# Late-row projections at the start, feed-forward pairs inside the recurrence, and another order of weight loads in a fused attention and feed-forward kernel

## The chip, the cores and the metric

The kernel runs on one core of a Trainium2 chip. The metric is device time in microseconds, as the median of several runs. Times inside the kernel come from one execution that was recorded by the hardware profiler; they count from the start of its span. The engines are TensorE (PE, with its weight loads PEld), VectorE (DVE), ScalarE (ACT), GpSimd (POOL) and SyncE (SP), which issues most of the DMAs.

## What is computed

A layer norm, an attention with a small memory that is handed from segment to segment, a residual, a second layer norm, a gated feed-forward part and a second residual. S = 2048 rows of width 640, 32 heads of 128, segments of 32 rows, 8 memory rows, feed-forward width F = 1728, all in bf16.

```python
def A(x, mem0, Wq, Wk, Wv, Wo, seg_len):              # x is the normalised input
    mem = mem0
    for s in range(64):
        h = concat([mem, x[:, 32*s:32*s+32]])         # 8 + 32 rows
        q, k, v = (einsum('btd,dhe->bhte', h, w) for w in (Wq, Wk, Wv))
        p = softmax(where(mask, q @ k.T * 128**-0.5, -1e9))
        o = einsum('bhte,hed->btd', p @ v, Wo)
        mem = o[:, :8]                                # the next segment needs this
        outs.append(o[:, 8:])
    return concat(outs)

def B(x, W_gate, W_up, W_down):
    gate = x @ W_gate
    return ((gate * (gate > 0)) * (x @ W_up)) @ W_down

h   = x + A(layernorm(x), ...)
out = h + B(layernorm(h), ...)
```

## The kernel before

**Order.** Every instruction is recorded by `add(engine, function, r=keys read, w=keys written)` and every DMA by `dma(...)`. `solve` turns the keys into semaphore waits; each engine then runs its own instructions in the recorded order. So the order of the source is the order of each queue, and an instruction that waits holds up all that stand behind it on its engine. DMAs go to SyncE's queue unless another engine is named. A key such as `("Wdone", 1)` stands for the last use of a weight matrix, after which its memory holds something else. `dma` issues at L349, DMA transposes at L372.

**The opening.** The weights W (Q, K and V, 15 chunks of 1 MB, in the order K, Q, V) and then Wo (8 loads) are read into SBUF. Meanwhile TensorE projects what it has: for K and Q three passes over each chunk (rows of segments 0 and 1, first group of late rows, memory and rows of segment 0), for V two (`first_values`). `keep_busy(n)` (L967) is n dummy matmuls into a bank that nothing reads. After the V chunks comes segment 0, and then the V projection of one more group of late rows into `Ve[0]`.

**The recurrence.** Steps 1 to 63 each do one segment: project the 8 memory rows with 24 of its own rows to K, Q and V (`project`: 40 products of 32 x 512 for each matrix, four of them side by side on TensorE's column groups, L411), scores (L507), softmax, values for the memory rows (`pv_mem`, L560), the output projection of the memory rows in two parts (L623 and L606) and their transposition into the next step's input. The values of the other rows (`pv_x`, L695) follow one step later. The last 8 rows of each segment, called late rows here, don't fit the 32-column pass; they are projected for four segments at once, one matrix a step, in `extra_units`: in steps r = 0, 1, 2 of each group of four the matrices K, Q, V go to `Ke`, `Qe`, `Ve` of the next group (two buffers each; buffer 1 of all three lies in `ends`). For the group of segments 58 to 61 these are steps 54, 55 and 56. The projection is cut into parts that fill places where TensorE would wait (`filler`).

**Feed-forward pairs inside the recurrence.** The first 512 rows are normalised and transposed early and kept in DRAM (`xn2_d`). In steps 58, 59 and 60, where no late rows are left to project, `early_product` computes one pair each (128 columns of gate and of up for the 512 rows, ten products of 128 x 512, L835), and stores the result in DRAM (`hx_d`). NE = 3 is their number. Rows lie in `ends`, the gate weights in `xt`, the up weights in `xl`.

**Splits.** `fill_of(s)` says how many of a step's projection matmuls are cut in two halves of 256 columns or load their weights again. This changes the number of TensorE's instructions in a step, not what is computed.

**The last part.** When the recurrence ends, the memory of W takes the feed-forward weights (`Wg`, `Wu`, `Wd`, the 64 tail columns `Wt`), rows and products. The pieces of `Wg` and `Wu` are listed in `pieces` by column groups and are loaded one by one by `load_piece(key)`, which waits for `("Wdone", 0)` and the key that is given; `load_down(n, p)` loads three row chunks of `Wd` and waits for the chunk NE + p of `hT`. Four blocks of 512 rows follow. A block has 13 pairs and a tail (`gate_up`, L835, L931, tail L944), then two pairs of down products (L1207, L384, L1220). Block 0 takes its first NE chunks of `hT` from `hx_d`; its next four pairs lie between the remains of steps 62 and 63, the rest behind. Rows of the next block are read, added to the attention (`ln2_front`, VectorE) and transposed by DMA (`ln2_back`) while a block runs.

## Time and profile before

| what | us |
|---|---|
| median of 3 runs | 995.79 (995.68 to 996.4) |
| the profiled execution, its time | 996.75 |
| its span | 995.0 |
| opening, up to the first output projection of segment 0 (L623) | 47.91 |
| output projection (L623) of step 1, of step 2 | 66.39, 78.59 |
| output projection of step 62 | 802.23 |
| first pair of block 0 after the recurrence's products (L835) | 810.75 |
| first down product of block 0 (L1207) | 842.93 |
| first pair of block 1 (L931) | 858.08 |

A step is 12.05 us in the mean ((802.23 - 66.39) / 61 = 12.06), and a block 44.25 us (858.08 to 902.32). The granted TensorE clock is 1.00 in nearly all stretches.

The table is read by stages: up to about 41 us the DMA engines are full with weights (share 1.0 at 411 to 425 GB/s), then come 62 steps in which TensorE is never idle for more than 0.1 us after step 2, then a stretch from 805 to 858 us in which weights are loaded again, and three equal blocks.

### The profile page before, as it was taken

What the parts mean: (1) busy time and instruction counts of PE and PEld (TensorE: products, weight loads), DVE (VectorE), ACT (ScalarE), POOL (GpSimd) and SP (SyncE); (2) the same over time, 40 slices, a digit from 0 to 9 for tenths busy, and PEclk for the clock granted to TensorE, in tenths of its full rate; (3) what the DMA queues carried; (4) which work ended last, traced back from release to release, by engine and by line L of the source; (5) the groups of instructions that cost most, each with busy time, mean ns of one, the idle gap of its engine ahead of it and who ended that gap; (6) DMA issues with size and microseconds to landing.
All of it is one profiled execution on the core that took longest, in us unless ns stands there. A gap on an engine that the chain in (4) does not pass through costs nothing.

```text
span 995.0 us, 56316 instructions
## 1 busy us (share of the span) xinstructions
PE 968.9 (97%) x26093; PEld 530.3 (53%) x24848; DVE 711.5 (72%) x1856; ACT 521.7 (52%) x1324; POOL 167.6 (17%) x412
## 2 busy tenths in 40 slices
PE   4799999999999999999999999999999999999998
PEld 1145555555555555555555655656565564444443
DVE  2468787878887887888788878787877865545332
ACT  1356666666666666666666666656665542122120
POOL 7011202021312130213022202021210010000000
PEclk9999999999999999999999999999999999999999
DMA  9941112121222122212212131112123259613100
GB/s 369 416 142 36 51 32 54 28 54 50 59 45 54 48 54 42 55 53 49 48 47 54 48 55 41 44 46 41 40 62 79 78 146 267 143 20 97 24 14 27
DMA packets 79105, 77.40 MB, mean 78 GB/s; under 512 B 45322, under 2 KB 64786, under 8 KB 76946
## 3 DMA queue, kind: packets, MB, share of 16 engines
q1 hardware_dynamic: 77136, 72.84, 26.4%
q8 instruction: 200, 3.28, 1.4%
q10 hardware_dynamic: 1730, 0.96, 0.4%
q14 instruction: 39, 0.32, 0.1%
HBM read 39.91 MB, written 7.74 MB: 48 GB/s over the span
## 4 chain that ended last, share of the span: by engine, by line
PE 94%; DMA 3%; DVE 1%; SPq 1%; issue 0%; ACT 0%; POOL 0%; DVEq 0%; ACTq 0%; POOLq 0%
PE ps L411 47%; PE ps L931 10%; PE ps L384 8%; PE ps L606 7%; PE ps L623 7%; PE ps L666 4%; PE ps L1207 3%; DMA W<-in_A_Wv_dram 3%; PE ps L507 2%; PE ps L695 2%; PE ps L560 2%; PE ps L835 2%; SPq L349 1%; PE ps L944 0%; PE ps L1220 0%
## 5 line engine op out<-in xcount | busy, mean ns | idle before, releaser
L411 PE MATMUL ps<-W,act_r 128*32 128x512 bf16 (+1 forms) x8301 | 453.8, 358 | 1.2 <-DVE act_r L647 0.8
L411 PEld LDWEIGHTS ps<-W,act_r 128*32 128x32 bf16 x8301 | 212.5, 96 | 165.9 <-DVE act_r L647 31.6
L435 ACT ACTIVATE tok<-ps 128x512 bf16<-128x512 f32 x186 | 107.2, 594 | 56.5 <-PE ps L411 48.6
L411 PE MATMUL ps<-W,act_e 128*32 128x512 bf16 x1152 | 112.8, 384 | 6.6 <-DMA W<-in_A_Wv_dram 4.1
L430 DVE STREAM_TRANSPOSE Ko<-tox 128x512 bf16<-128x512 bf16 x128 | 89.6, 701 | 40.9 <-ACT tox L435 40.7
L435 ACT ACTIVATE tox<-ps 128x512 bf16<-128x512 f32 x134 | 79.7, 598 | 65.1 <-PE ps L411 44.9
L586 DVE STREAM_TRANSPOSE oT<-tox 128x512 bf16<-128x512 bf16 x128 | 94.5, 738 | 0.0
L430 DVE STREAM_TRANSPOSE Qo<-tok 128x512 bf16<-128x512 bf16 x124 | 85.4, 689 | 0.8
L606 PE MATMUL ps<-Wo,oT 128*32 128x160 bf16 x4032 | 81.5, 233 | 0.0
L623 PE MATMUL ps<-Wo,oT 128*32 128x320 bf16 x2016 | 79.8, 299 | 0.6 <-DVE rm L570 0.6
L384 PE MATMUL ps<-W,act_e 128*32 128x512 bf16 x808 | 79.8, 385 | 0.0
L606 PEld LDWEIGHTS ps<-Wo,oT 128*32 128x32 bf16 x4032 | 70.3, 97 | 11.1 <-DVE oT L580 3.1
L435 ACT ACTIVATE Vp<-ps 128x512 bf16<-128x512 f32 x127 | 75.1, 592 | 0.5 <-ACT Vp L435 0.5
L636 ACT ACTIVATE SA<-TA 64x40 f32<-64x40 f32 x126 | 29.5, 234 | 75.2 <-DVE TA L634 74.5
L959 ACT ACTIVATE g<-ps 128x512 bf16<-128x512 f32 x49 | 28.3, 593 | 75.8 <-PE ps L931 74.1
L523 ACT ACTIVATE Pm<-ps 128x64 bf16<-128x64 f32 x126 | 28.2, 224 | 73.6 <-PE ps L507 73.6
L960 DVE TENSOR_TENSOR hT<-g,ps 128x512 bf16<-128x512 bf16 x49 | 33.6, 687 | 40.3 <-PE ps L931 35.5
L623 PEld LDWEIGHTS ps<-Wo,oT 128*32 128x32 bf16 x2016 | 52.7, 96 | 16.7 <-DVE rm L570 1.3
L580 DVE STREAM_TRANSPOSE oT<-om 128x128 bf16<-128x128 bf16 x126 | 39.0, 309 | 31.2 <-ACT om L572 31.1
L507 PE MATMUL ps<-Qo,Ko 128*32 128x40 bf16 x2048 | 61.0, 181 | 0.0
L507 PEld LDWEIGHTS ps<-Qo,Ko 128*32 128x32 bf16 x2048 | 46.2, 94 | 25.6 <-DVE Qo L430 18.1
L1207 PE MATMUL ps<-Wd,hT 128*128 128x320 bf16 (+4 forms) x225 | 57.9, 299 | 1.7 <-DVE hT L954 1.7
(131 smaller groups left out, 1441.1 us busy)
## 6 DMA issues: line engine op xcount, KB each, us to landing
VM<-Vp SPq DMA_DIRECT2D x126, 65.0 KB
VM<-Vp SPq DMA_DIRECT2D x63, 130.0 KB
W<-in_A_Wk_dram SPq DMA_DIRECT2D x5, 1024.0 KB
W<-in_A_Wq_dram SPq DMA_DIRECT2D x5, 1024.0 KB
W<-in_A_Wv_dram SPq DMA_DIRECT2D x5, 1024.0 KB
Wo<-in_A_Wo_dram SPq DMA_DIRECT2D x8, 640.0 KB
attn_d<-wtok SPq DMA_DIRECT2D x248, 7.5 KB
xt<-in_A_x_dram SPq DMA_DIRECT2D x16, 160.0 KB
```

The lines of the kernel that those rows point to most:

```text
L384: return pe.add_instruction(mybir.InstMatmult(name=nc.get_next_instruction_name(), engine=mybir.EngineType.PE, ins=[pe.lower_ap(rhs), pe.l ...
L411: ins = pe.matmul(*b, start=(c == ends[0]), stop=(c == ends[1]), skip_group_check=True)
L430: add("dve", lambda v: v.transpose(dst[:, 16 * i:16 * i + 16, 0:32], tok[t][:, :].rearrange("p (h f) -> p h f", f=32)), r=tok_keys(t), w=keys)
L435: add("act", lambda a: a.activation(dst, src, ACTF.Copy), r=r, w=w)
L507: i = pe.matmul(bank((P0, P1)[hf])[q:q + 32, o:o + 40], (Ko if a == 0 else Ke[p])[:, h, :], Qo[:, h, :], start=True, stop=True, skip_group ...
L580: add("dve", lambda v: v.transpose(ap(oT[par], 160 * hf, [[40, 4], [320, 4], [1, 8]]), ap(om, 128 * hf, [[1, 4], [4, 32]])), r=[("om", hf) ...
L586: add("dve", lambda v, kh=kh: v.transpose(ap(oT[p], 160 * kh + M, [[320, 4], [40, 4], [1, 32]]), ap(tox, 128 * kh, [[256, 4], [1, 4], [4, ...
L606: i = pe.matmul(bank(bk)[32 * gg:32 * gg + 32, 0:160], src[:, hb, 0:32], w[:, gg], start=(hb == CH[16 * halves[0]]), stop=(hb == CH[-1]), ...
L623: i = pe.matmul(bank(bk)[32 * q:32 * q + 32, 0:320], src[:, hb, 0:32], w, start=(n == 0), stop=(n == 7), skip_group_check=True)
L666: ins = pe.matmul(bank(bk)[32 * q:32 * q + 32, 0:320], src[:, hb, 0:32], w[:, 2 * (q % 2):2 * (q % 2) + 2], start=(i == 0), stop=(i == 15) ...
L931: ins = pe.matmul(bank(bk), w[:, c, lo:lo + 128], xn2T[par][:, c, :], start=(c == 0), stop=(c == DC - 1))
L1207: i = pe.matmul(*a, start=(j == 0), stop=(j == FC - 1), skip_group_check=True)
```

## The change

Five things change.

1. K and Q of the late rows of segments 58 to 61 are projected in the opening (`next_pass`, two passes of 40 products of 32 x 512). For this the 32 rows are loaded into `xl` ahead of the Q weights, normalised and transposed on TensorE; the results are flipped into `Ve[0]` and `oTe`, saved to DRAM (`next_d`) and loaded into `Ke[0]`, `Qe[0]` in step 56. The ten dummy matmuls go. The load of block 1's rows into `xl` and the copies into `Ve[0]` move behind the saves, and ones are set in `Ve[0]` again.
2. Steps 54 and 55 compute feed-forward pairs instead: NE = 5, `EARLY_STEPS` is (54, 55, 58, 59, 60). Their rows lie in `Ke[0]`, `Qe[0]`, `Ve[0]`, the up weights in `at`. V of these late rows stays in step 56.
3. With NE = 5 there are four column groups of `Wg` and `Wu` and not five. Pieces and `Wd` loads in the last part wait for the end of W's use alone, and stand earlier. The tail weights are loaded once each and copied on POOL into the second order.
4. In a tail the second half of `g1` has a key of its own.
5. `fill_of`: step 1 has 126 in place of 31, step 54 0 in place of 7, step 55 25 in place of 52.

```diff
-    NE = 3
+    NE = 5
+    next_d = [nc.dram_tensor(f"next{i}_d", [128, 32 * H], BF16) for i in range(2)]
...
+            if j == 1 and c == DC - 1:
+                for e in range(4):
+                    t0 = SEG * (NSEG - 6 + e) + RID
+                    dma(xl[M * e:M * e + M, :], x_ap[t0:t0 + M, :], w=[("xl", e)])
...
-    ln1_load(1, xl, ("xl",))
+    for n, (t, ks) in enumerate(((Ve[0], [("Ve", 0, i) for i in range(2)] + [("Ve1", 0)]), (oTe, [("oTe", q) for q in range(4)]))):
+        held_saves.append((n, t, ks))
...
+    row_moments(xl, ("xl", 0), 32, [("xl", e) for e in range(1, 4)])
+    row_std(32)
+    row_scale(xl, ("xl", 0), 32, xl, ("xl",))
...
+            if j == 0 and c == DC - 2:
+                transpose_rows(xl, ("xl",), 32, P3)
+                copy_op("dve", a2, chunks_of(bank_bf(P3)[:, 0:D])[:, :, 0:32], [B(P3)], k2[:2])
...
-    first_values(range(2))
+    def next_pass(n):
+        j, bks, t = ((1, (P0, P1), 2), (0, (T0, T1), 0))[n]
+        for i in range(2):
+            project(a2, k2, j, (i,), (bks[i],))
+        for i in range(2):
+            to_tok(bks[i], t + i, "act")
+            add("dve", lambda v, i=i: v.transpose(next_home(n)[:, 16 * i:16 * i + 16, :],
+                                                  tok[t + i][:, :].rearrange("p (h f) -> p h f", f=32)),
+                r=tok_keys(t + i), w=held_saves[n][2])
...
+    first_values((0,))
+    next_pass(0)
+    first_values((1,))
+    next_pass(1)
...
-    keep_busy(10)
     first_values((3,))
...
+    wo_pass(0, P3, (1,), (3,))
+    keep_busy(3)
+    for n, t, ks in held_saves:
+        dma(next_d[n][:, :], (ap(Ve[0], 0, [[1, 32 * H]]), oTe[:].rearrange("p h t -> p (h t)"))[n], r=ks, w=[("next", n)])
+    ln1_load(1, xl, ("xl",))
+    to_act_split(1, P3)
     for i in range(2):
         to_v(BQ[i], Ve[0], i, ("Ve", 0), "act")
-    wo_pass(0, P3, (1,), (3,))
-    keep_busy(3)
-    to_act_split(1, P3)
+    add("pool", lambda p: p.memset(ap(Ve[0], Dh, [[VW, 8], [1, VW - Dh]]), 1.0), w=[("Ve1", 0)])
     row_stats(xl, ("xl",), n_rows(1))
...
-            if (s - 2) // 4 + 1 == (NSEG - 2) // 4:
-                return early_product(s, r)
+            if s in EARLY_STEPS:
+                return early_product(s)
...
-        n = {1: 31, 2: 8, 57: 39, 58: 0, 59: 27, 60: 40, 61: 39, 62: 50, 63: 0}.get(s, FILL[s % 4])
+        n = {1: 126, 2: 8, 54: 0, 55: 25, 57: 39, 58: 0, 59: 27, 60: 40, 61: 39, 62: 50, 63: 0}.get(s, FILL[s % 4])
...
+            elif s == NSEG - 8:
+                for n, t in enumerate((Ke[0], Qe[0])):
+                    dma(t[:].rearrange("p h t -> p (h t)"), next_d[n][:, :], r=[("next", n)],
+                        w=[(("Ke", "Qe")[n], 0, i) for i in range(2)])
+                add("pool", lambda p: p.memset(ap(Ve[0], Dh, [[VW, 8], [1, VW - Dh]]), 1.0),
+                    w=[("Ve1", 0), ("Ve", 0, 0), ("Ve", 0, 1)])
...
-            if s == NSEG - 7:
-                early_weights(0, 0)
+            if s in (NSEG - 11, NSEG - 7):
+                early_weights(s + 1, 0)
                 G.ops[-1].after = first_exp
-                early_rows(2, 4)
+                early_rows(s > NSEG - 8, 2, 4)
...
-        r = [("Wdone", 1), ("hT", 0, NE + p)]
+        r = [("Wdone", 1)]
...
-    load_piece(("VM", 0, 3))
-    load_piece(("hT", 0, NE))
+    for _ in range(4):
+        load_piece(("Wdone", 0))
     rows(P3, s % 2, s - 1)
     gate_up(0, NE + 1)
+    for n in range(2):
+        load_down(n)
...
+    dma(hT[0][:, 0:NE, :], hx_d[:, :, :], r=[("Wdone", 2)] + [("hx", n) for n in range(NE)],
+        w=[("hT", 0, n) for n in range(NE)])
+    load_down(2)
     gate_up(0, NE + 3)
-    load_piece(("hT", 0, NE + 3))
-    dma(hT[0][:, 0:NE, :], hx_d[:, :, :], r=[("Wdone", 2), ("hT", 0, NE + 3)] + [("hx", n) for n in range(NE)],
-        w=[("hT", 0, n) for n in range(NE)])
-    load_down(0, 3)
-    load_down(1, 3)
+    for q, src in enumerate((B_W_gate, B_W_up)):
+        dma(Wt[:, 0, :, FR * q:FR * q + FR], src[:, FM:F].rearrange("(c p) f -> p c f", p=128), r=[("Wdone", 0)],
+            w=[("Wt", q, 0)])
+        add("pool", lambda o, q=q: o.tensor_copy(Wt[:, 1, :, FR * (1 - q):FR * (2 - q)], Wt[:, 0, :, FR * q:FR * q + FR]),
+            r=[("Wt", q, 0)], w=[("Wt", q, 1)])
+    load_down(3)
     rows(P2, (s + 1) % 2, s)
     ln2_load(5)
+    load_down(4)
...
-            if b == 0 and p in (8, 9):
+            if b == 0 and p in (7, 8):
                 load_piece(("hT", 0, j))
                 load_piece(("hT", 0, j))
             if b + 1 < NBLK:
-                fronts, backs = ((4, 6), (7, 9)) if b == 0 else ((1, 3, 5, 7), (3, 5, 7, 9))
+                fronts, backs = ((4, 6), (6, 8)) if b == 0 else ((1, 3, 5, 7), (3, 5, 7, 9))
```

More of the change, by code (lines that the diff above doesn't have):

```diff
@@ L748, in ln2_back @@
         flip_rows(xn2T[par][:, :, 128 * u:128 * u + 128], xt2[u], ("xt2", u), ("xn2", par, u))
+    held_saves = []
     x0 = oTe[:].rearrange("p h t -> p (h t)")[:, 0:D]
@@ L790, in build_kernel @@
     OB = {1: (BQ, (T0, T1), (P2, P3)), 0: ((P0, P1), BQ, (T0, T1)), 2: ((P2, P3), BQ)}
+    a2, k2 = act_r[1][:, 2], [("act", 1, 2, "m"), ("act", 1, "x", 2), ("act", 1, "x")]
     for j in (1, 0):
@@ L808, in first_values, with next_home @@
                 project(a, ks, 2, (0, 1), bks, (c,))
-    first_values(range(2))
+    def next_pass(n):
[7 more added lines that the diff above has]
+                r=tok_keys(t + i), w=held_saves[n][2])
+    def next_home(n):
+        return (ap(Ve[0], 0, [[32, H], [1, 32]]), oTe)[n]
+    first_values((0,))
+    next_pass(0)
+    first_values((1,))
+    next_pass(1)
     EC = 128 * NE
-    GROUPS = ((EC, EC + 256), (EC + 256, EC + 512), (EC + 512, EC + 1024), (EC + 1024, FM), (0, EC))
+    GROUPS = [(EC, EC + 256), (EC + 256, EC + 512), (EC + 512, EC + 1024), (0, EC)]
+    if EC + 1024 < FM:
+        GROUPS.insert(3, (EC + 1024, FM))
     pieces = [(t, n, src, g, lo, hi) for g, (c0, c1) in enumerate(GROUPS)
               for n, (t, src) in enumerate(((Wg, B_W_gate), (Wu, B_W_up)))
-              for lo, hi in (((0, 3), (3, DC)) if g in (2, 4) else ((0, DC),))]
+              for lo, hi in (((0, 3), (3, DC)) if g in (2, len(GROUPS) - 1) else ((0, DC),))]
     def group_of(j):
@@ L829, in build_kernel, with flat_half @@
     END_KEYS = [("Ke", 1, 0), ("Ke", 1, 1), ("Qe", 1, 0), ("Qe", 1, 1), ("Ve", 1, 0), ("Ve", 1, 1), ("Ve1", 1)]
-    XHOME = [(ends[:, 512 * c:512 * c + 512], END_KEYS[c]) for c in range(DC)]
-    HOME, HKEY = ends[:, 64 * H + 4 * VW + 8:64 * H + 4 * VW + 520], END_KEYS[DC]
+    VHOME = 4 * VW + 8
+    def flat_half(t, i):
+        return t[:].rearrange("p h t -> p (h t)")[:, 512 * i:512 * i + 512]
+    XHOME = [[(flat_half((Ke[0], Qe[0])[c // 2], c % 2), (("Ke", "Qe")[c // 2], 0, c % 2)) for c in range(4)] +
+             [(ap(Ve[0], 0, [[1, 512]]), ("Ve", 0, 0))],
+             [(ends[:, 512 * c:512 * c + 512], END_KEYS[c]) for c in range(DC)]]
+    HOME = [(ap(Ve[0], VHOME, [[1, 512]]), ("Ve", 0, 1)), (ap(Ve[1], VHOME, [[1, 512]]), ("Ve", 1, 1))]
     def by_groups(pe, dst, w, x, c):
@@ L837, in by_groups, with early_rows, early_tile, early_weights @@
         return ins
-    def early_rows(lo, hi):
-        dma(ends[:, 512 * lo:512 * hi].rearrange("p (c t) -> p c t", t=512), xn2_d[:, lo:hi, :],
-            r=[("xn2_d", u) for u in range(4)], w=END_KEYS[lo:hi] + ([("Ve1", 1)] if hi == DC else []))
-    def early_weights(j, q):
-        t, k, src = ((xt, ("xt",), B_W_gate), (xl, ("xl",), B_W_up))[q]
+    def early_rows(q, lo, hi):
+        ks = [XHOME[q][c][1] for c in range(lo, hi)] + ([("Ve1", q)] if hi == DC else [])
+        if q:
+            dst = ends[:, 512 * lo:512 * hi].rearrange("p (c t) -> p c t", t=512)
+        elif hi == DC:
+            dst = XHOME[0][4][0].rearrange("p (c t) -> p c t", t=512)
+        else:
+            dst = (Ke[0], Qe[0])[lo // 2][:].rearrange("p h t -> p (h t)").rearrange("p (c t) -> p c t", t=512)
+        dma(dst, xn2_d[:, lo:hi, :], r=[("xn2_d", u) for u in range(4)], w=ks)
+    def early_tile(s, q):
+        return ((xt, ("xt",)), (at, ("at",)) if s < NSEG - 7 else (xl, ("xl",)))[q]
+    def early_weights(s, q):
+        (t, k), src = early_tile(s, q), (B_W_gate, B_W_up)[q]
+        j = EARLY_STEPS.index(s)
         dma(chunks_of(t[:, :]), src[:, 128 * j:128 * j + 128].rearrange("(c p) f -> p c f", p=128), w=[k])
-    def early_product(s, n):
+    EARLY_STEPS = (NSEG - 10, NSEG - 9, NSEG - 6, NSEG - 5, NSEG - 4)
+    def early_product(s):
+        n, hp = EARLY_STEPS.index(s), int(s >= NSEG - 6)
+        home, hkey = HOME[hp]
         def mul(q, chunks):
-            t, k = ((xt, ("xt",)), (xl, ("xl",)))[q]
+            t, k = early_tile(s, q)
             def f(pe):
                 for c in chunks:
-                    ins = by_groups(pe, bank(BQ[q]), chunks_of(t[:, :])[:, c, :], XHOME[c][0], c)
+                    ins = by_groups(pe, bank(BQ[q]), chunks_of(t[:, :])[:, c, :], XHOME[hp][c][0], c)
                 return ins
-            add("pe", f, r=[k] + [XHOME[c][1] for c in chunks], w=[B(BQ[q])])
+            add("pe", f, r=[k] + [XHOME[hp][c][1] for c in chunks], w=[B(BQ[q])])
         def part(m):
@@ L861, in evac @@
         def evac():
-            add("act", lambda a: a.activation(HOME, bank(BQ[0]), ACTF.Relu), r=[B(BQ[0])], w=[HKEY])
-            add("dve", lambda v: v.tensor_tensor(HOME, HOME, bank(BQ[1]), ALU.mult), r=[B(BQ[1]), HKEY], w=[HKEY])
-            dma(hx_d[:, n, :], HOME, r=[HKEY], w=[("hx", n)])
+            add("act", lambda a: a.activation(home, bank(BQ[0]), ACTF.Relu), r=[B(BQ[0])], w=[hkey])
+            add("dve", lambda v: v.tensor_tensor(home, home, bank(BQ[1]), ALU.mult), r=[B(BQ[1]), hkey], w=[hkey])
+            dma(hx_d[:, n, :], home, r=[hkey], w=[("hx", n)])
         return part, evac
@@ L951, in gate_up @@
                 add("act", lambda a, r0=r0, r1=r1, sl=sl: a.activation(g1[gi][r1:r1 + FR, sl], bank(bg)[r0:r0 + FR, sl],
-                                                                       ACTF.Relu), r=[B(bg)], w=[("g1", gi)])
+                                                                       ACTF.Relu), r=[B(bg)], w=[("g1", gi, e) if e else ("g1", gi)])
                 h = hT[par][:, j, :].rearrange("p (u e t) -> p e u t", e=2, t=128)[r1:r1 + FR, e]
@@ L956, in gate_up @@
                     bank(bg)[r1:r1 + FR, sl].rearrange("p (u t) -> p u t", t=128), ALU.mult),
-                    r=[B(bg), ("g1", gi)], w=[("hT", par, j)])
+                    r=[B(bg), ("g1", gi)] + [("g1", gi, 1)] * e, w=[("hT", par, j)])
             return
@@ L1048, in build_kernel @@
             held, parts = fill_of(s)
-            if NSEG - 6 < s < NSEG - 3:
-                early_weights(s - NSEG + 6, 1)
+            if s in (NSEG - 10, NSEG - 9, NSEG - 5, NSEG - 4):
+                early_weights(s, 1)
+            elif s == NSEG - 8:
[4 more added lines that the diff above has]
+                    w=[("Ve1", 0), ("Ve", 0, 0), ("Ve", 0, 1)])
             elif s == NSEG - 3:
@@ L1146, in build_kernel @@
         filler(1)
-        if s == NSEG - 7:
-            early_rows(0, 2)
-            early_rows(4, DC)
-            early_weights(0, 1)
-        elif NSEG - 6 <= s < NSEG - 4:
-            early_weights(s - NSEG + 7, 0)
+        if s in (NSEG - 11, NSEG - 7):
+            early_rows(s > NSEG - 8, 0, 2)
+            early_rows(s > NSEG - 8, 4, DC)
+            if s == NSEG - 7:
+                early_weights(s + 1, 1)
+        elif s in (NSEG - 10, NSEG - 6, NSEG - 5):
+            early_weights(s + 1, 0)
         norm_mem(s, 1)
@@ L1260, in down_pair, with load_down @@
             down_store(b, u + q, o[q])
-    def load_down(n, p):
+    def load_down(n):
         lo, hi = 3 * n, min(3 * n + 3, FC - 1)
-        r = [("Wdone", 1), ("hT", 0, NE + p)]
+        r = [("Wdone", 1)]
         dma(Wd[:, lo:hi, :], B_W_down[128 * lo:128 * hi, :].rearrange("(j p) d -> p j d", p=128), r=r, w=[("Wd", n)])
@@ L1295, in build_kernel @@
     late_o(s)
-    load_piece(("hT", 0, NE + 1))
     gate_up(0, NE + 2)
     ln2_load(4)
-    load_piece(("hT", 0, NE + 2))
-    load_piece(("hT", 0, NE + 2))
-    gate_up(0, NE + 3)
-    load_piece(("hT", 0, NE + 3))
-    dma(hT[0][:, 0:NE, :], hx_d[:, :, :], r=[("Wdone", 2), ("hT", 0, NE + 3)] + [("hx", n) for n in range(NE)],
-        w=[("hT", 0, n) for n in range(NE)])
-    load_down(0, 3)
-    load_down(1, 3)
+    if len(GROUPS) > 4:
+        load_piece(("Wdone", 0))
+        load_piece(("Wdone", 0))
+    dma(hT[0][:, 0:NE, :], hx_d[:, :, :], r=[("Wdone", 2)] + [("hx", n) for n in range(NE)],
+        w=[("hT", 0, n) for n in range(NE)])
+    load_down(2)
+    gate_up(0, NE + 3)
+    for q, src in enumerate((B_W_gate, B_W_up)):
[4 more added lines that the diff above has]
+    load_down(3)
     rows(P2, (s + 1) % 2, s)
     ln2_load(5)
+    load_down(4)
     woe_pass(P3, range(16))
@@ L1320, in build_kernel @@
                 gate_up(b, j)
-            if b == 0 and p == 4:
-                for q, src in enumerate((B_W_gate, B_W_up)):
-                    for e in range(2):
-                        r0 = FR * (q ^ e)
-                        dma(Wt[:, e, :, r0:r0 + FR], src[:, FM:F].rearrange("(c p) f -> p c f", p=128),
-                            r=[("Wdone", 0), ("hT", 0, j)], w=[("Wt", q, e)])
             if b == 0 and p in (4, 5):
                 ln2_load(p + 2)
-            if b == 0 and 4 <= p < 7:
-                load_down(p - 2, p)
-            if b == 0 and p == 6:
+            if b == 0 and p == 5:
                 dma(h_rows[0][:, :, :], h_d[:, :].rearrange("(u p) d -> p u d", p=128), r=[("h_d", u) for u in range(4)] +
                     [("Wdone", 1), ("hT", 0, j)], w=[("h", 0, u) for u in range(4)])
-            if b == 0 and p in (8, 9):
+            if b == 0 and p in (7, 8):
                 load_piece(("hT", 0, j))
```

## The prediction

> **What bounds the kernel now.** I read the page first: the busy shares, then the chain that ended last. TensorE is busy 97% of the span and carries 94% of the chain, so a change pays only if it takes TensorE work off the path or closes one of TensorE's few gaps. The line of queue 8 (instruction loads) is used for a rival below.

> ```profile
> span 995.0 us, 56316 instructions
> PE 968.9 (97%) x26093; PEld 530.3 (53%) x24848; DVE 711.5 (72%) x1856; ACT 521.7 (52%) x1324; POOL 167.6 (17%) x412
> q8 instruction: 200, 3.28, 1.4%
> PE 94%; DMA 3%; DVE 1%; SPq 1%; issue 0%; ACT 0%; POOL 0%; DVEq 0%; ACTq 0%; POOLq 0%
> ```

> Then TensorE's timeline at both ends; a bracket is idle time before the line and what ended it. In the opening it waits for each 1 MB chunk of the V weights and fills one wait with ten dummy matmuls (L967 and the L384 after it).

> ```profile
> 33.62 0.40 PE L411 MATMUL ps<-W,act_e 128*32 128x512 bf16 x4 [1.09 <-DMA W<-in_A_Wv_dram]
> 36.01 0.40 PE L411 MATMUL ps<-W,act_e 128*32 128x512 bf16 x4 [1.33 <-DMA W<-in_A_Wv_dram]
> 36.98 0.39 PE L967 MATMUL ps<-W 128*128 128x512 bf16 x1
> 37.21 2.11 PE L384 MATMUL ps<-W 128*128 128x512 bf16 x9
> 40.98 0.40 PE L411 MATMUL ps<-W,act_e 128*32 128x512 bf16 x4 [1.67 <-DMA W<-in_A_Wv_dram]
> ...
> 840.00 1.26 PE L944 MATMUL ps<-xn2T,Wt 128*128 128x256 bf16 x10
> 842.93 0.30 PE L1207 MATMUL ps<-Wd,hT 128*128 128x320 bf16 x1 [1.68 <-DVE hT L954]
> ```

> The last line is TensorE's only gap after step 2. VectorE is named, but the first down product does not read the tail rows; it reads hT 0 to 11 and Wd pieces 0 to 3. In the trace's landing records the last part of Wd piece 3 lands at 842.84, 0.09 us before the matmul: this is a late DMA. SyncE's timeline shows that piece issued only at 836.80.

> Third, VectorE's timeline around 57 us, where step 1 begins: it runs nearly without a break from here to 66 us and TensorE waits for it twice (0.94 us at 66.16, 0.84 at 69.67). So what delays L353 delays everything.

> ```profile
> 57.30 0.20 DVE L647 TENSOR_TENSOR act_r<-TBf,SA 128x40 bf16<-128x40 f32 x1
> 57.77 0.89 DVE L353 BATCH_NORM_STATS2 st<-xl 128x6 f32<-128x320 bf16 x2 [0.27 <-issue]
> 59.57 0.45 DVE L367 TENSOR_SCALAR xl<-xl,mv,rs 128x640 bf16<-128x640 bf16 x1 [0.67 <-ACT rs L360]
> 59.98 1.32 DVE L430 STREAM_TRANSPOSE Ko<-tox 128x512 bf16<-128x512 bf16 x2
> ```

> Last, busy times by stretch. A step is measured from one first L623 matmul to the next: the first two rows end in steps 55 and 56, which hold a projection of late rows, the next two in 59 and 60, which hold a feed-forward pair in the same place. The columns are TensorE, weight loads, VectorE, ScalarE, POOL, clock, DMA share, GB/s; the later rows give only the last three.

> ```profile
> 705.93:717.98 12.05, 12.05 (x394) 7.21 (x373) 9.98 (x26) 7.51 (x19) 1.12 (x3) 1.00 0.11 29
> 717.98:730.03 12.05, 12.05 (x394) 7.14 (x374) 10.04 (x26) 7.51 (x19) 1.10 (x3) 1.00 0.11 30
> 754.13:766.18 12.05, 12.05 (x382) 7.21 (x376) 9.50 (x25) 7.02 (x18) 1.13 (x3) 1.00 0.27 67
> 766.18:778.21 12.03, 12.03 (x386) 7.16 (x382) 9.55 (x25) 7.02 (x18) 1.10 (x3) 1.00 0.28 68
> ...
> 816.00:820.00 4.00, 1.00 0.50 146
> 820.00:824.00 4.00, 1.00 0.78 230
> 824.00:828.00 4.00, 1.00 0.98 279
> 828.00:832.00 4.00, 1.00 1.02 358
> ```

> **Part 1: two pairs leave block 0.** With NE=5 the last part computes 8 full pairs of block 0, not 10. Six pairs there run from 827.04 to 840.00: 12.96 / 6 = 2.16 us each, with no gap. Two pairs: -4.32 us.

> **Part 2: the gap before the down products.** Before, each weight piece waits on SyncE's queue for a finished hT chunk; the DMA engines are half idle at 816 to 820. After, four pieces and Wd 0, 1 are issued behind the VM copies (814.4), and Wd 2 and 3 wait for no hT. Ahead of and with Wd 3 stand 1.31 MB pieces, 1.97 MB Wd, 0.66 MB hT rows, 0.33 MB x and attention rows, 0.16 MB tail weights: 4.4 MB. At 325 GB/s (mean of 822 to 832) from 816.5 that is 830. Two of the four tail loads remain; they ran with others at 132 GB/s in 832 to 836, so I add 2 us, and 1.3 us for the slowest DMA engine (it is so much behind at 55 us): Wd 3 lands at 833.5. TensorE ends the tail matmuls at 841.26 - 4.32 = 836.9. VectorE has hT 11 by 834.4 (it comes ahead of the second row front, which ends at 837.3) and hT 12 at 838.0, wanted at 840.1. So the gap goes: -1.68 us (ends: 0 and -1.68). Next due is block 1 at 836.9 + 15.15 = 852.1: its last transposed rows. VectorE finishes the last two row fronts at about 841.6 and 844.4; issue to landing was 4.5 us before, so 849, 3 us early. POOL's two copies of tail weights have that engine free. The finer g1 key shortens the tail's VectorE work behind TensorE: 0.

> **Part 3: steps 54 and 55.** A pair has the same ten 512-column products as the projection it replaces; the rows above say 12.05 against 12.05 and 12.03 (and steps 54 and 58, by their L623 starts, 12.19 and 12.15). The loads go where steps 57 to 59 have theirs. Tightest is the up weight in step 54: it stands on SyncE's queue behind the stores whose issue ends at 700.5, POOL has freed `at` at 698.0, issue to landing takes 2.7 to 3.6 us (the loads of 746.1 and 759.86), so 704.1; TensorE wants it at 705.7. Behind it wait the VM copies, wanted a step later. I take 0 (ends -0.1 and +1). The two reloads and the memset of step 56 have 12 us on queues that are 11% busy: 0. Step 1's fill only halves matmuls; steps with fills 56 and 52 last as long (12.06, 12.05), and VectorE sets step 1: 0 (ends 0 and +1).

> **Part 4: the opening.** Two projections are 20 groups of four at 0.215 us: 4.3 us. They lie in the waits for weights: 1.09 + 1.33 + 1.67 us idle and 2.34 us of dummy matmuls, which go. K starts after chunk 0 (34.5 to 36.7), chunk 1 moves to 36.7 to 37.5, Q takes 37.5 to 39.7; chunk 3 lands at 40.9. Cost 0, with 1.2 us to spare; without cover it would be 4.3. ScalarE and VectorE have four copies (0.6 us) and flips (0.7 us) more, in a stretch where ScalarE idles 7.6 us up to 42.34 and VectorE 6.65 up to 42.66: 0. The 32 extra rows are 41 KB ahead of the Q and V weights: at 424 GB/s +0.1 us.

> **Part 5: the rows of block 1 come later.** Two stores of 262 KB now stand ahead of `xl` on SyncE's queue, behind Wo. In the landing records the last parts are at 56.19 (Wo), 56.59 (xl) and 58.55 (the 0.79 MB of ends_d, so 403 GB/s). The stores add 2 x 0.65 us: xl at 57.9, with the 0.1 at 58.0; L353 starts at 58.1 instead of 57.77: +0.3 us (ends 0 and +5.7, see the third rival). ScalarE's V copies wait for the first store (56.9) and end at 58.1, before L358 needs it at 59.2.
> [...]

> **Sum:** -4.32 - 1.68 + 0 + 0.1 + 0.3 = -5.6 us. The profiled execution (span 995.0, time 996.75) would have a span of 989.4. The median of the runs shown is 995.79, 0.96 under the profiled one; the difference carries over: **990.2 us**.

> **Rivals.** *The DMA engines set the tail.* Their share is 0.9 to 1.46 from 836 to 852. If the same bytes end no earlier, Wd 3 still lands at 842.8, both gains are lost and only the opening's 0.4 remains: 996.2. Against it: the idle share at 816 to 824 and two strided loads fewer. Half of it gives 993.
> *The instruction stream loses its phase* (slower). 51,319 TensorE instructions (matmuls, weight loads, 378 others) in 200 packets on queue 8 are 257 each. TensorE's weight loads idle 183 times, 48.2 us in all, for nothing but "issue", 0.26 us each and about three times a step; no matmul gap goes with it now. If one a step came to lie on the matmuls' path, 61 x 0.26 = +15.9 us, less 5.6: 1006. It decides from 0.09 us a step. Against it: in the two programs' instruction lists TensorE's count at each step from 1 to 53 and from 56 on is exactly 256 higher after, one packet; that is what step 1's fill does.
> [...]
> *The stores drain slowly.* If each took the 3.4 us that the hx_d store of 759.46 takes to land, one after the other, xl would come at 56.2 + 6.8 + 0.4 = 63.4, L353 5.7 us late: 995.9, no change. A quarter of it: 991.5. Against: 403 GB/s of ends_d.

> **Chances.** Forecast 0.77; a part of the stores' delay (991.5) 0.09; half of the DMA rival (993) 0.05; all of it, or of the stores (996), 0.05; phase 0.04. What this measurement can tell from no change is about 0.2%, 2.0 us. Faster is the first three, 0.91; same 0.05; slower 0.04. The range goes from 989.0 (the sum, 0.3 less in the opening, 0.9 for the 0.4 us that runs differ and small gaps) to 993.2, which takes in the partial cases.

> **What would show it.** Right: block 0's down products start about 6 us earlier against step 62 and with no gap ahead; L353 starts 0.2 to 0.6 us later against the Wv chunk; steps 54 and 55 keep 12.05 to 12.2. Wrong: a DMA gap at the first down product or at block 1's first pair; TensorE idle at the up product of step 54; ScalarE held at the V copies past 59 us; a longer step all along.

## The result, and the profile after

The seven runs of the changed kernel have a median of **993.00 us** (990.55 to 993.68), seven of the kernel before on the same chip 995.79 (995.26 to 996.40). The ratio is 0.9965, with a 95% interval of 0.9953 to 0.9977. The forecast was 990.2 with a range of 989.0 to 993.2.

The profiled execution has a span of 989.0 (forecast 989.4) and a time of 990.74, 6.0 under the profiled one of before (forecast 5.6). The seven times lie apart: 990.55, 990.74, 991.77 and then 993.00 to 993.68. So there are two questions: did the profiled 6.0 come from where the prediction put them, and what are the 2.5 us that four of the seven runs take on top. The lines that answer to those of before, from the page of the changed kernel first:

```profile
span 989.0 us, 56556 instructions
PE 964.6 (98%) x26166; PEld 532.7 (54%) x24973; DVE 713.7 (72%) x1861; ACT 522.5 (53%) x1326; POOL 169.6 (17%) x416
q8 instruction: 201, 3.29, 1.4%
PE 93%; DMA 4%; DVE 1%; SPq 1%; issue 0%; ACT 0%; POOL 0%; DVEq 0%; ACTq 0%; POOLq 0%
```

TensorE is busy 4.3 us less: the two pairs. Its timeline in the opening and at the first down product, then VectorE's where step 1 begins (start, length, idle time before and what ended it in brackets):

```profile
33.18 0.40 PE L412 MATMUL ps<-W,act_e 128*32 128x512 bf16 x4 [1.09 <-DMA W<-in_A_Wv_dram]
34.04 2.34 PE L412 MATMUL ps<-W,act_r 128*32 128x512 bf16 x40
36.20 0.40 PE L412 MATMUL ps<-W,act_e 128*32 128x512 bf16 x4
37.06 2.35 PE L412 MATMUL ps<-W,act_r 128*32 128x512 bf16 x40
41.10 0.40 PE L412 MATMUL ps<-W,act_e 128*32 128x512 bf16 x4 [1.69 <-DMA W<-in_A_Wv_dram]
...
836.57 1.26 PE L998 MATMUL ps<-xn2T,Wt 128*128 128x256 bf16 x10
837.66 0.30 PE L1271 MATMUL ps<-Wd,hT 128*128 128x320 bf16 x1
```

```profile
57.79 0.89 DVE L354 BATCH_NORM_STATS2 st<-xl 128x6 f32<-128x320 bf16 x2 [0.23 <-DMA xl<-in_A_x_dram]
59.59 0.45 DVE L368 TENSOR_SCALAR xl<-xl,mv,rs 128x640 bf16<-128x640 bf16 x1 [0.67 <-ACT rs L361]
```

The two new projections (the x40 groups) fill the wait for the second chunk and part of that for the third. The down product follows the tail matmuls without a bracket. L354 now does wait for the `xl` transfer, but starts 0.02 us later than before, no more.

Marked off by the same events in both traces, the 6.0 us are:

| stretch | before | after | difference |
|---|---|---|---|
| start to step 62's first row product | 802.23 | 803.45 | +1.22 |
| from there to the first full pair of block 0 | 24.81 | 24.55 | -0.26 |
| the full pairs of block 0 (6 and 4) | 12.96 | 8.57 | -4.39 |
| tail matmuls and gap, to the first down product | 2.93 | 1.09 | -1.84 |
| from there to VectorE's last operation | 148.94 | 148.94 | 0.00 |
| from there to the end (last store) | 3.16 | 2.41 | -0.75 |

(The first full pair of after lacks one matmul record; its start is put 0.16 us, one matmul, before the first recorded one.) The second row of -0.26 was not followed up. The last row is not a quicker store: in both kernels the last store lands 1.5 us after VectorE's last operation. Behind it SyncE works through its waits for 24 DMA semaphores (the loop over `G.dma_end` at the end of the kernel), 0.06 us apart in its records. The last store has the fifth of them before and the eighteenth after, so 19 waits stand behind it before and 6 after, about 0.78 us less.

The +1.22 is not the opening: step 1's first row product is at 66.45 instead of 66.39. Counted by the first row product (L624) at which they end, steps 12, 28 and 44 take 12.35 to 12.37 us instead of 12.06, together 0.9; steps 54 and 56 take 0.15 more. The timeline of the changed kernel, all engines, shows ahead of 199.73, where step 12 ends, what the 0.3 is:

```profile
188.97 0.40 POOL L596 COPY oTe<-oT 128x256 bf16<-128x256 bf16 x1
189.22 0.48 ACT L637 ACTIVATE SA<-TA 64x40 f32<-64x40 f32 x2 [1.22 <-DVE TA L635]
...
190.13 0.27 POOL L639 TENSOR_TENSOR SA<-SA,TA 128x40 f32<-128x40 f32 x1 [0.76 <-DVE TBf L647]
...
190.50 0.20 DVE L648 TENSOR_TENSOR act_r<-TBf,SA 128x40 bf16<-128x40 f32 x1 [0.38 <-POOL SA L639]
...
190.76 0.51 PE L412 MATMUL ps<-W,act_r 128*32 128x512 bf16 x8 [0.17 <-DVE act_r L648]
```

POOL's addition (L639) reads `SA`; ScalarE is done with it at 189.70. The addition starts 0.43 us after that. In the kernel before, the same two stand at 189.64 and 189.77, 0.13 apart. Everything behind it, down to TensorE, shifts by the 0.3. This addition is POOL's 197th recorded instruction (its waits counted), and the same place in steps 28 and 44 its 325th and 453rd, 128 further each time; each time a packet of 8,192 bytes of queue 14 goes by beside it (190.8, 385.3, 578.6). The page calls that queue an instruction queue, with 39 packets; the four engines other than TensorE have 5,037 recorded instructions, 129 for each packet. In the kernel before, the 197th is the copy of `Qo` at 200.77, 0.3 us late as well (10.73 us after POOL's last operation instead of 10.42), for which nobody waits.

### The profile page after: what moved, and what is told of

It is laid out like the page before. It is cut to its first block, busy times and chain, and to the rows that moved or that the text cites. A ratio compares the mean times of both kernels' runs of the same rounds, so it can differ in the third digit from the quotient of the medians.

```text
span 989.0 us, 56556 instructions
## 1 busy us (share of the span) xinstructions
PE 964.6 (98%) x26166; PEld 532.7 (54%) x24973; DVE 713.7 (72%) x1861; ACT 522.5 (53%) x1326; POOL 169.6 (17%) x416
## 4 chain that ended last, share of the span: by engine, by line
PE 93%; DMA 4%; DVE 1%; SPq 1%; issue 0%; ACT 0%; POOL 0%; DVEq 0%; ACTq 0%; POOLq 0%
PE ps L412 47%; PE ps L985 9%; PE ps L385 7%; PE ps L607 7%; PE ps L624 7%; PE ps L667 4%; PE ps L1271 3%; DMA W<-in_A_Wv_dram 2%; PE ps L508 2%; PE ps L696 2%; PE ps L875 2%; PE ps L561 2%; DMA xl<-in_A_x_dram 2%; SPq L350 1%; PE ps L998 0%
## 5 line engine op out<-in xcount | busy, mean ns | idle before, releaser
L412 PE MATMUL ps<-W,act_r 128*32 128x512 bf16 (+1 forms) x8410 | 458.6, 357 | 1.7 <-DVE act_r L648 1.3
L412 PEld LDWEIGHTS ps<-W,act_r 128*32 128x32 bf16 x8410 | 215.6, 96 | 168.4 <-DVE act_r L648 32.1
L412 PE MATMUL ps<-W,act_e 128*32 128x512 bf16 x1104 | 108.0, 383 | 5.2 <-DMA W<-in_A_Wv_dram 2.8
L624 PE MATMUL ps<-Wo,oT 128*32 128x320 bf16 x2016 | 79.8, 299 | 0.5 <-DVE rm L571 0.5
L385 PE MATMUL ps<-W,act_e 128*32 128x512 bf16 x776 | 76.6, 384 | 0.0
L624 PEld LDWEIGHTS ps<-Wo,oT 128*32 128x32 bf16 x2016 | 52.7, 96 | 16.7 <-DVE rm L571 1.2
L516 POOL COPY Qo<-Qe 128x256 bf16<-128x256 bf16 x32 | 14.1, 442 | 259.9 <-DVE oT L581 249.5
```

What stands on the lines that cost most here:

```text
L385: return pe.add_instruction(mybir.InstMatmult(name=nc.get_next_instruction_name(), engine=mybir.EngineType.PE, ins=[pe.lower_ap(rhs), pe.l ...
L412: ins = pe.matmul(*b, start=(c == ends[0]), stop=(c == ends[1]), skip_group_check=True)
L624: i = pe.matmul(bank(bk)[32 * q:32 * q + 32, 0:320], src[:, hb, 0:32], w, start=(n == 0), stop=(n == 7), skip_group_check=True)
```

## The experiments

The first four runs ask whether POOL's late instruction explains the long runs, and what the load order of the last part is worth.

**The changed kernel again, and POOL moved against its blocks.** One run repeats the kernel as it is, two add instructions at POOL's start (`L331` of after, `L330` of before):

```
-    add("pool", lambda p: p.memset(mbd[:], 0.0), w=[("mbd",)])
+    for _ in range(4):          # 3 in the kernel before
+        add("pool", lambda p: p.memset(mbd[:], 0.0), w=[("mbd",)])
```

> The changed kernel once more, unchanged, to see whether its times stay spread (990.55 to 993.68) and to have a second trace. Theory A (POOL's instruction stream): three times, every 16 steps, POOL's L639 starts 0.3 us late on the path to the next step's input; the same three places are late again, and where the run is slower they are later than 0.3 us each. Theory B (DMA): the spread comes from loads in the opening or in the last part; then a slower run has its extra time in a gap at a Wv chunk, at the first down product or at a block's start. Times 990.5 to 993.7 by both.

> The changed kernel with three more memsets on POOL at the start, which do nothing new: they move the place of every later POOL instruction in its stream by three. Theory A: the late place falls on the copy L516, which has 6 us to spare; steps 12, 28 and 44 take 12.06 and not 12.36, span about 988.1, median about 990, spread no more than 1.2 us like the kernel before. Theory B: steps unchanged or not, the median stays at 993 and the spread at 3 us.

> The kernel before with two more memsets on POOL at the start: by the count of its POOL instructions the late place moves from the copy L515 to the addition L638 of the step ahead. Theory A: three steps become 0.3 us longer or more, time 996.7 to 999 and a spread like that of the changed kernel. Theory B: 995.8 as before, spread 1.1.

Measured: the repeat 991.31 (990.61 to 994.00; ratio 0.9964, 0.9952 to 0.9976), so a second set of runs has the same two groups. With three more memsets 990.93 (989.87 to 996.33; 0.9962, 0.9948 to 0.9976); steps 12, 28 and 44 are 12.06 us each. The kernel before with two more memsets 996.82 (995.43 to 997.57; 1.0009, 1.0001 to 1.0018); its three steps are now 12.35. POOL's and TensorE's timelines of the first of the two:

```profile
189.60 0.27 POOL L640 TENSOR_TENSOR SA<-SA,TA 128x40 f32<-128x40 f32 x1 [0.20 <-ACT SA L638]
...
190.23 1.27 PE L413 MATMUL ps<-W,act_r 128*32 128x512 bf16 x25
```

The bracket before the addition falls to 0.20 and TensorE has none. Both directions agree: POOL's 197th, 325th and 453rd instructions are some 0.3 us late, whatever they are, and cost that much when they are this addition. The change has eight more POOL instructions, two of them ahead of step 12, and so put it there. The spread of the times stayed, so this is not what the long runs lose.

The profile of the kernel before with two more memsets also bears on Part 2. Its tail matmuls start 0.85 us later than before (840.85 instead of 840.00), yet its first down product only 0.29 later, and the gap ahead of it is smaller by the rest:

```profile
843.22 0.30 PE L1208 MATMUL ps<-Wd,hT 128*128 128x320 bf16 x1 [1.11 <-DVE hT L955]
```

The last part of Wd piece 3 lands at 843.13 there, again 0.09 us ahead of the product. So this gap ends with the load, whenever TensorE gets there.

**The old load order in the new kernel.**

```
-        r = [("Wdone", 1)]
+        r = [("Wdone", 1), ("hT", 0, NE + p)]      # load_down(n, p) again
...
-    for _ in range(4):
-        load_piece(("Wdone", 0))
+    load_piece(("VM", 0, 3))
+    load_piece(("hT", 0, NE))                     # one piece, hT and Wd behind each chunk, as before
```

> The changed kernel with the weight loads of the last part where the kernel before has them, each behind a finished hT chunk. If the gap ahead of the down products was a late load and the new order takes it away (as predicted): Wd chunk 3 is issued after hT 10, at about 834, lands at about 839.5, and TensorE idles about 2 us at 837.7, so the time is 1.5 to 3 us above that of the changed kernel. If the order of loads does nothing and the gap came from the tail's VectorE work: no gap, same time as the changed kernel.

Measured: 996.33 (994.82 to 997.82; 1.0003, 0.9994 to 1.0012): all of the gain is gone. TensorE's timeline:

```profile
838.22 1.26 PE L998 MATMUL ps<-xn2T,Wt 128*128 128x256 bf16 x10
841.97 0.30 PE L1271 MATMUL ps<-Wd,hT 128*128 128x320 bf16 x1 [2.49 <-DMA Wd<-in_B_W_down_dram]
```

I had expected 1.5 to 3 us. The first down product is 4.31 us later than in the changed kernel: 2.66 by this gap, 0.81 already at step 62 (0.45 in the opening and 0.49 in steps 54 and 58, less 0.13 elsewhere), and the rest in between, 0.46 of it in one gap at 819.04. With the old order TensorE starts the tail matmuls 1.8 us sooner than before (838.22 against 840.00) and then waits for much the same transfer (the last part of the Wd piece lands at 841.88, against 842.84 before). The gain of Part 1 needs the new order.

**Where the long runs lose.** Four theories were then open (they are named in the first of these expectations). Besides the unchanged kernel: the last four weight pieces two chunks earlier (`if b == 0 and p in (5, 6)` for `(7, 8)`), the load of `xl` ahead of the two stores, and the kernel before with only the new load order of the last part, NE=3.

> The changed kernel, unchanged. Its times lie in two groups so far (about 990.6 and 993 to 994, span 989 and 991.5); the one profile of it was of the lower group. Open: what the upper 2.5 us are. Theory S1: block 1's first pair waits for its last transposed rows (they landed 2.9, 2.1 and 1.0 us before they were needed in three profiles). S2: the xl rows of block 1, behind the two stores of the opening, land late in some executions and TensorE waits at step 1. S3: a Wd piece lands late and the gap ahead of the first down product is back. S4: TensorE's instruction blocks arrive late in steps that also move weights (0.1 to 0.5 us each seen in steps 54, 58 and 61). Expected: again 990.6 to 994; if the profile falls in the upper group, S1 shows as a TensorE gap at 853, S2 as L354 later than 60, S3 as a gap at 837.7, S4 as several small gaps without a cause.

> The changed kernel with the last four weight pieces issued two chunks earlier (behind chunks 5 and 6 of block 0's pairs, not 7 and 8), ahead of block 1's transposes on SyncE's queue. S1: the last transposed rows land 1.5 to 2 us earlier (848.5), and the upper group of times goes: all runs 990 to 991.5. S2, S3, S4: the spread stays, 990.5 to 994, the median within 0.2% of the changed kernel. A cost is possible where the pieces now hold up the last Wd piece or the rows: under 0.5 us.

> The changed kernel with the load of block 1's first rows put ahead of the two stores of the opening. My prediction put the stores' delay at 0.3 us (0.02 was measured, xl landing at 57.8): L354 starts at 57.7 or, if nothing else holds it, at 57.2, and the time is 0 to 0.5 lower. S2: the upper group goes, all runs 990 to 991.5. S1, S3, S4: the spread stays.

> The kernel before with only the load order of the last part changed (three early pairs, no new work in opening and steps). By my prediction's Part 2 the 1.68 us gap ahead of the first down product goes and nothing else changes: profiled span 993.3, median 994.1. Rival from the run with the old order (4.3 us in its span): the gap there was 2.5 us and hit a kernel that reaches it 4.3 us earlier, so the order alone is worth only 1 to 1.7 here. S3: the times spread over 2.5 us or more, 994 to 997. S1, S2: spread of about 1 us as in the kernel before.

Measured: unchanged 991.12 (990.75 to 993.82), early pieces 992.12 (991.16 to 994.53), `xl` first 991.53 (990.57 to 993.51); ratios 0.9964, 0.9968 and 0.9963, each about 0.001 either way. The spread stayed in both edits, so neither block 1's rows alone nor the stores make it. The medians show no gain with `xl` first. Its profile does, beside that of the first repeat, whose opening ran alike (the first L624 at 47.45 and 47.47). VectorE's line of the repeat, then VectorE's and TensorE's of the kernel with `xl` first:

```profile
58.08 0.89 DVE L354 BATCH_NORM_STATS2 st<-xl 128x6 f32<-128x320 bf16 x2 [0.95 <-DMA xl<-in_A_x_dram]
...
57.05 0.88 DVE L354 BATCH_NORM_STATS2 st<-xl 128x6 f32<-128x320 bf16 x2
66.04 1.27 PE L624 MATMUL ps<-Wo,oT 128*32 128x320 bf16 x32
```

With the stores ahead L354 waits 0.95 us for `xl`, and step 1's first row product comes at 66.48; with `xl` first it waits for nothing and the product comes at 66.04. So the 0.02 us of the first profile, whose opening ran 0.5 us later, are not what the stores cost in every execution.

The profile of the kernel with the early pieces fell on a long execution (span 992.8, time 994.53). Up to 836 it issues the same as the changed kernel, so the stretch before that can be read for it. Its chain of waits (start, length, what held TensorE), and its busy times by 4 us (TensorE, weight loads, VectorE, ScalarE, POOL, clock, DMA share, GB/s):

```profile
819.50 4.00 PE ps L875 x72
823.50 1.62 issue
825.12 0.61 PE ps L875 x8
825.74 4.08 PE ps L667 x120
829.81 1.52 issue
831.33 0.46 PE ps L667 x8
```

```profile
820.00:824.00 4.00, 3.50 (x68) 1.49 (x56) 2.93 (x6) 1.82 (x4) 0.40 (x1) 1.00 1.03 336
824.00:828.00 4.00, 2.88 (x80) 2.14 (x84) 0.69 (x1) 0.04 (x1) 0.00 (x0) 1.00 1.05 396
828.00:832.00 4.00, 2.32 (x65) 1.45 (x55) 0.48 (x1) 0.56 (x2) 0.00 (x0) 1.00 0.96 256
```

TensorE stands still for 3.1 us in two places (the three short runs of this kernel, 991.16 to 991.41, are 3.1 to 3.4 us under this one), each in the middle of one operation (after 12 of 20 matmuls, after 56 of 64), where it waits for no semaphore. The two places are exactly 128 matmuls and 128 weight loads apart. The trace of the changed kernel has 51,519 TensorE instructions to 201 packets of queue 8, 256 each, here called a block, and the long run's records of that queue fit: a packet runs from 822.79 to 823.71, TensorE goes on at 825.12; the next from 828.84 to 829.98, TensorE goes on at 831.33. That is 1.41 and 1.35 us after the packet's end. In the unchanged kernel's run beside it the packets start at 819.21 and 825.43, and no matmul waits.

The records read as if a block is fetched while the one before it runs. In the unchanged kernel's run TensorE comes to the first matmuls of three successive blocks at 817.5, 823.16 and 827.78 (the first is where the kernel with the old load order stopped for 0.46 us, the others are the two places above). So it works through 256 instructions in 4.6 to 5.7 us, since most of its matmuls here are 32 columns wide (84 matmuls from 820 to 824 in the changed kernel, 36 with wide ones in the last experiment), and each packet starts 1.7 and 2.3 us after the block before it is begun. In the long run the same two start 5.1 and 3.7 us after (817.7 and 825.12; the expectations below put 817.7 at 818.2, which is too late). If a block has to be there when the one before it is used up, then by my estimate from these numbers a packet of 1 us and the 1.4 us after it leave 2.2 to 3.3 us to wait for the DMA engines, and they are full from 819 to 831 (share 1.04 to 1.05).

The same reading holds for the small irregularities elsewhere. From 780 to 832 us TensorE stops for 0.1 us or more without a semaphore twelve times in eight traces, these two places among them (gaps at a missing matmul record left out), and all twelve stops end 1.3 to 1.6 us after the end of a packet of queue 8. They also stand at nearly one place of the count: the matmuls and weight loads up to the stop, divided by 256, leave 105 at 780 us and 84 at 831, and 84 to 104 between. Three more delays of 0.1 to 0.3 us in steps 54 and 58 end 1.8 to 1.9 us after a packet. The 0.24 us in the kernel with three memsets, for one, end after a packet that ends at 778.55:

```profile
780.08 1.01 PE L608 MATMUL ps<-Wo,oT 128*32 128x160 bf16 x47 [0.24 <-issue]
```

In the kernel before, the same dense stretch (818 to 827) met DMA shares of 0.5 to 0.98, as the prediction's rows show.

The new load order alone gave 995.58 (994.54 to 997.67; 0.9999, 0.9990 to 1.0008). Its profile (span 993.6) has no gap ahead of the first down product:

```profile
840.26 1.25 PE L944 MATMUL ps<-xn2T,Wt 128*128 128x256 bf16 x10
841.35 0.30 PE L1207 MATMUL ps<-Wd,hT 128*128 128x320 bf16 x1
```

So the order takes the gap away in the execution that was profiled, but the median does not fall. Part of that lies in which executions were profiled: the one of the kernel before is a long one (996.75, 0.96 over its median), so the median execution need not have the whole 1.68 us to lose. The spread says nothing here, since the kernel before spread as far in its 17 runs beside this one (994.75 to 997.74). That late blocks give the rest back was not seen in a trace of this kernel.

**Less traffic in that stretch.** Wd 0 and 1, `hT` and what stands behind them wait for chunk NE+3 of `hT`; in the three kernels: the changed one, the one with three memsets, and the load order alone.

```
     gate_up(0, NE + 1)
-    for n in range(2):
-        load_down(n)
...
-    dma(hT[0][:, 0:NE, :], hx_d[:, :, :], ...)
-    load_down(2)
     gate_up(0, NE + 3)
+    load_down(0, [("hT", 0, NE + 3)])              # added to r
+    load_down(1)
+    dma(hT[0][:, 0:NE, :], hx_d[:, :, :], ...)
+    load_down(2)
```

> The changed kernel, where the first down weights, the pair rows hT and everything behind them on SyncE's queue wait for chunk NE+3 of hT (about 824.5) instead of following the weight pieces at 819. S4, as one long profile showed it (TensorE stood still twice in the middle of a group of matmuls, 1.62 and 1.52 us, 128 matmuls and 128 weight loads apart, and the packet of queue 8 came 4.7 us after the block before it was begun): between 819 and 824 the DMA engines are free again when TensorE asks for its next block, so the upper group of times goes: 990.5 to 991.5, median 990.8, no TensorE gap between 816 and 837, Wd 3 landing near 834. If the spread stays (990.5 to 994), the backlog of the DMA engines is not what delays the blocks, or the blocks at 825 to 830 are the ones that matter. If Wd 3 lands after 837.7 a gap at the first down product takes its place.

> The same with the three extra memsets on POOL, which took 0.9 us out of steps 12, 28 and 44: 0.9 less than the kernel with the wait alone, median 989.9, 989.5 to 990.7. If S4 falls, the spread of 989.9 to 993.5 stays.

> The kernel before with the load order of the last part and the same wait. Without the wait the median was 995.58 (994.5 to 997.7), although its profile (span 993.6) no longer had the gap ahead of the first down product. S4: the spread goes and the 1.7 us of Part 2 show in the median: 993.9 to 994.6. If S4 falls: 995.5 again, spread 3 us.

Measured: 992.46 (991.12 to 993.90; 0.9969), 991.38 (989.60 to 993.36; 0.9956) and 995.22 (994.57 to 996.80; 0.9997, 0.9988 to 1.0005). This missed. The stalls in the dense stretch shrink but do not go: 0.20 us at 819.03 in the first, 0.39 at 823.22 in the second. Ahead of each the DMA engines are busy without the held loads (share 0.81 to 0.92 from 815 to 817 in the first, 1.08 to 1.13 from 818 to 821 in the second). And another wait comes in. TensorE's timeline of the first, at block 1:

```profile
854.06 0.45 PE L1284 MATMUL ps<-Wd,hT 64*128 64x320 bf16 x4
855.92 1.24 PE L985 MATMUL ps<-xn2T,Wg 128*128 128x512 bf16 x5 [1.42 <-DMA xn2T<-xt]
```

The rows of the last segments stand behind the held loads on SyncE's queue: the store of `attn_d` that landed at 832.4 in the changed kernel lands at 837.8, and block 1's transposed rows come 1.4 us too late. The median did not fall, so this doesn't tell how much of the long runs the blocks make.

**Fewer instructions in that stretch.** Pairs NE+2 and NE+3 use five 128-column matmuls a product instead of twenty of 32 columns; no transfer is moved, and the three memsets stay.

```
-                    if b == 0 and j < NE + 4:
+                    if b == 0 and j < NE + 2:
                         ins = by_groups(...)
```

> The changed kernel with the three memsets on POOL, and with the pairs NE+2 and NE+3 of block 0 as five full 128-column matmuls a product instead of twenty of 32 columns. The load order is untouched; only TensorE's instructions in the stretch with full DMA engines are fewer: 120 of the 256 of one block. By the long profile's positions the block begun at 818.2 then lasts until 825.4 instead of 823.0, and the next until about 839 instead of 827.3. S4 (blocks that arrive late because the DMA engines are full): both stalls go, no TensorE gap between 816 and 837, and the last part adds nothing to the spread: median 990.0, 989.5 to 991.3; the same kernel without this had a median of 990.9 and ran from 989.9 to 996.3. A cost of up to 0.3 us is possible where 32- and 128-column matmuls change places. If S4 falls, the spread stays and the median is 990.9 to 991.2. If only a part of the long runs goes, the rows of block 1 (the gap of 1.4 us at its first pair in the kernel with the wait) are a second place.

Measured: **990.59** (989.63 to 991.95; 0.9949, 0.9936 to 0.9963), the best of all, but 0.6 over the expected median and with one time above the expected 991.3. TensorE's timeline, and the busiest stretch:

```profile
820.00 1.24 PE L986 MATMUL ps<-xn2T,Wu 128*128 128x512 bf16 x5
821.08 1.24 PE L986 MATMUL ps<-xn2T,Wg 128*128 128x512 bf16 x5
822.15 1.24 PE L986 MATMUL ps<-xn2T,Wu 128*128 128x512 bf16 x5
823.33 2.36 PE L668 MATMUL ps<-Wo,oT 128*32 128x320 bf16 x64
825.51 2.35 PE L668 MATMUL ps<-Wo,oTe 128*32 128x320 bf16 x64
```

```profile
820.00:824.00 4.00, 4.00 (x36) 1.92 (x38) 3.00 (x6) 1.82 (x4) 0.40 (x1) 1.00 1.05 356
824.00:828.00 4.00, 3.86 (x116) 2.87 (x106) 0.60 (x2) 0.52 (x2) 0.00 (x0) 1.00 1.10 373
```

36 matmuls in 820 to 824 do what 84 did in the changed kernel, at the same DMA share, and there is no stall. No packet of queue 8 begins between 817.68 and 827.86. The pairs cost no more time (1.08 us a product either way), and no change of width shows as a gap (from 822.15 the last wide group and the change to 32 columns take 1.18 us). The five times hold none over 992. Four of nine of the same kernel with narrow pairs were over 992; five clean draws at that rate would come by luck about once in twenty times ((5/9)^5 = 0.05), and the line at 992 was drawn after the times were known, so they support the explanation without settling it. In this profile steps 54 and 62, in which early loads run, are 0.4 us longer each; that late blocks do this was not shown, and what the run of 991.95 lost was not seen.

## Why the prediction was right, and where it was not

- **Part 1, two pairs, -4.32**: right; 8.57 us instead of 12.96 are -4.39.
- **Part 2, the gap, -1.68**: right in the profiled execution (-1.84 by the starts, the last tail matmul now overlapping the next product), and the reason too: with the old order the gap is 2.49 us and ends at a Wd landing. Wd 3 landed at 831.74 (forecast 833.5), block 1's rows at 850.11 (849). The order alone gained nothing in the median, though (ratio 0.9999): part of the price lay elsewhere, below.
- **Part 3, steps 54 and 55, 0**: within its bounds, +0.1 and 0, with another 0.06 in step 56. The loads were in time; the delays seen in steps 54 and 58 (0.1 to 0.3 us) end 1.8 to 1.9 us after a packet of queue 8.
- **Part 4, the opening, 0 and +0.1**: the two projections fill the waits as laid out. Step 1's first row product is 0.06 us later in all, with Part 5, but over the other profiles with the stores in this place it lies between 66.25 and 66.97, so one execution doesn't resolve 0.1 us.
- **Part 5, `xl` behind the stores, +0.3**: the mechanism was right, and the size depends on the execution. In the first profile `xl` landed at 57.77 (forecast 58.0) and L354 moved by 0.02, because before it had already waited 0.27 us for nothing that the profile names (`xl` had landed at 56.59). In two other profiles it waited 0.95 and 0.84 us for `xl`, and the pair of profiles above gives 0.44 us at step 1's first row product. ScalarE's V copies wait for the first store, whose last part landed at 56.73 (forecast 56.9), and run from 56.81 for 1.08 us, to 57.89 (forecast 58.1). L368 moved by 0.02.
- **Not in the sum**: the 0.9 us in steps 12, 28 and 44. The reasons for the rival counted TensorE's instructions against their blocks, and not POOL's, where two more ahead of step 12 move the late one to the addition that TensorE waits for. Nor were the -0.26 and the -0.75 at the end in it. What the sum left out comes to +0.15 us (1.16 more from step 1 to step 62, less these two), so that the profiled 6.0 lies so near the forecast 5.6 is partly luck.
- **The step that failed** is "the difference carries over": the profiled execution's distance to the median. It was the right sum for an execution like the profiled one (990.74, 990.55, and 990.6 to 991.4 in 7 of the 11 repeats), but the median of the seven runs is 2.8 over the forecast. Over the three sets of the unchanged kernel ten of 18 executions take 990.55 to 991.77 and eight 993.0 to 994.0, with a median of 991.6, so the seven drew more long ones than the repeats (991.31 and 991.12), which are 1.1 and 0.9 over. The profile of before was of one of its long executions and that of after of one of its short ones, so the difference of the profiles is larger than that of the medians. I had the rival, the instruction stream, in the wrong place: I priced it per step, at 0.26 us, and closed it by counting. By the long profile, what counts is how fast TensorE uses up blocks (256 instructions in 4.6 to 5.7 us) where the DMA engines are full (share 1.03 to 1.05 from 820 to 828). In Part 2 I took "the DMA engines are half idle at 816 to 820" as room for loads. By my reading of that profile it was also what brought the blocks in time: with full engines two of them cost 1.62 and 1.52 us there.

What stays open: only one long execution of this load order was profiled, so that every run near 993 loses its time in the dense stretch is inferred from it. The rows of block 1 were 1.0 to 4.9 us early in the profiles of the changed kernel and its variants with unheld loads, and may come late in some of the others. The longest run of the kernel with three memsets, 996.33, has no explanation.

## What to carry to other kernels

Before packing loads into a stretch where the DMA engines look half idle, count the instructions that the engines execute there: here blocks of 256 TensorE instructions that were used up in 4.6 to 5.7 us came late in the one long execution that was profiled, where those engines were full (two stops of 1.62 and 1.52 us at a share of 1.03 to 1.05), and the same work in wide matmuls needed a quarter of the instructions. A stop in the middle of one operation, with no semaphore, is read by the instruction number and the packets of the instruction queue; look at the count of every engine on the path, not TensorE's alone. And a profile shows one execution: where the times of a kernel spread more than before, the sum is right for the profiled one and not yet for the median.
